# Half tiles for x, sooner loads of x, and w_v's last block in the Fourier tail of a fused FFT and expert kernel

## The chip, the cores and the metric

The kernel runs on one core of one Trainium2 chip. The metric is the time of one execution on the device in microseconds (us). A core has five engines with queues of their own: TensorE (PE, the matrix products), VectorE (DVE), ScalarE (ACT), GpSimd (POOL) and SyncE (SP), which here only issues DMAs. Each engine works through its own list in order, and waits on semaphores for the others.

## What is computed

```
X = np.fft.fft(np.fft.fft(x, axis=1), axis=2).real            # x [4, 3072, 256]
x_prev = X shifted by one place along the sequence
xk, xr = mu_k * X + (1 - mu_k) * x_prev, mu_r * X + (1 - mu_r) * x_prev
k = np.maximum(xk @ w_k, 0.0);  v = k * k @ w_v               # w_k [256, 1024], w_v [1024, 256]
r = 1.0 / (1.0 + np.exp(-(xr @ w_r)));  y = r * v             # w_r [256, 256]
h = y @ w_in;  out = (h - np.tanh(h)) @ w_out                 # w_in [256, 2048]
```

All arrays are handed over in float32, but the weights arrive as 64-bit words, which the kernel turns into float32 itself: that is the conversion of which this text speaks.

## The kernel before

**Stages.** A Fourier part (fft_phase, to about 93 us) leaves the transformed tokens in SBUF (tiles y). Phase 1 does the first expert layer for 12 blocks of 512 tokens, in 4 quads each: quad(1, ...) is a product of 2 by 2 blocks with seven instead of eight multiplications, each product made of three matmuls on split operands (mm3, L364 to L366). A quad has 7 products of the first kind (out tiles x, z, w) and, delayed by one quad, the products with w_v (out tiles o). Phase 2 does h and tanh in the same way.

**Fourier part.** x has 4 batches b of 3 pieces p, numbered here x0 to x11 (3b + p). load(b, p) (L102) fetches a piece into a tile xr with two halves, out of 3 buffers. For b below 2, one DMA on SP's queue brings both halves, and VectorE adds them (L146). For b from 2 on, SP's DMA (L110) brings the first, and a DMA on POOL's queue adds the second to it in flight (L111, "accumulating"), into half 0; half 1 of such a tile stays unused. fold_piece makes fe and fo on VectorE (L147, L148) and then issues the load of the piece three later. step1 multiplies fe and fo by the first matrix (PE L168), ScalarE spreads the result into E (L178); step2 (PE L193, ScalarE L196 to L201) and step3 (PE L234, L235, ScalarE L244, VectorE L257) make the tokens y. The loop over b and i interleaves step1 of one batch with step2 and step3 of the batch before.

**Conversion of weights.** convert (L402) yields a list of steps for each block: load of the raw words (SP, L411), absolute value (ScalarE, L433), and on VectorE the operations L421, L423, L425, L427, L429 and a sum (L437), or, for blocks that go to DRAM (wf), a store and an accumulating DMA (L444, L439). In the Fourier part four blocks of w_k (each followed by L500 to L509, which make TK), one of w_r and three of w_v stand in a list, work. more(b, i) (L286) takes steps from it: a table of rates for each b and i adds to due, and each whole number is one step. Before the last pass (b == 4) the rest of the list is emptied and the buffers of x and of the conversion are given up (fctx.close()).

**Slots.** In phase 1 and at the end of the Fourier part, side work is bound to slots: at(slot, ...) files functions, fill() runs those of the next slot. Numbering begins at -15 in the Fourier tail; quad 0 of phase 1 holds 6 fills and later quads 4, 16 slots a block. wv_task(q) gives a load of w_v's block q from wf into a tile of the 4 xk buffers, and a split: ScalarE casts it (L398) and POOL subtracts (L399). both_tasks makes the next block's left operands: d, k, the sums "+s1" to "+s4" on POOL (L669 to L672, on raw[0] to raw[3], the xk tiles) and their casts (L659) and low halves (L661). w_v's fourth block is converted in phase 1 itself (L816 to L818), the w_in blocks at places of START, the w_out blocks behind them.

**Within a quad** (L525): after the products x and z ScalarE copies s1, s2, s3; bend is ScalarE's relu (c<-z, L540), gate VectorE's square, hi the cast m (ScalarE L545), lo its low half (VectorE L547), each for four results 11, 22, 21, 12. extra() issues the product for r and gives back the sigmoid (L813), which reads the bank of x that the next quad writes first.

Of the kernel before, what the change touches and what calls it, by code (L numbers as in the profile page):

```python
# [7 lines left out]
F32 = mybir.dt.float32  # L8
# [4 lines left out]
B, S, D = 4, 3072, 256  # L13
T1, T2 = 128, 24
# [3 lines left out]
FOLDED = 2  # L18
# [69 lines left out]
def fft_phase(tc, x, f96_in, cst_in, swap, ypool, ys, work, first, hook, fill):  # L88
    nc = tc.nc
    V, A, G, T = nc.vector, nc.scalar, nc.gpsimd, nc.tensor  # L90
    ALU, ACT = mybir.AluOpType, mybir.ActivationFunctionType
    with tc.tile_pool(name="fc", bufs=1) as fc, ExitStack() as fctx, tc.tile_pool(name="fe", bufs=2) as fe, tc.tile_pool(name="fz", bufs=3) as fz, \
# [3 lines left out]
        work = work(fctx)  # L96
# [4 lines left out]
        xs = {}  # L101
        def load(b, p):  # L102
            rows = 5 if p == 2 else 4
            t = fx.tile([T1, 2, 5, D], F32, tag="xr", name=f"xr{b}_{p}")
            for c, n in FIRST[p] if b == 0 else ((0, rows),):
                src = x[:, b, :, 4 * p + c:4 * p + c + n]
                if b < FOLDED:
                    nc.sync.dma_start(out=t[:, :, c:c + n], in_=src.rearrange("k p c d -> p k c d"))
                else:
                    nc.sync.dma_start(out=t[:, 0, c:c + n], in_=src[0])  # L110
                    G.dma_start(out=t[:, 0, c:c + n], in_=src[1], accum_op=ALU.add)  # L111
            xs[b, p] = t
        zero = fc.tile([128, 128], F32, name="zero")
        V.memset(zero, 0.0)
        for b in range(B):
# [22 lines left out]
        def fold_piece(b, p):  # L138
            t = xs.pop((b, p))
            rows = 5 if p == 2 else 4  # L140
            e = fx.tile([T1, 5, 128], F32, tag="fe", name=f"fe{b}_{p}", bufs=2)
            o = fx.tile([T1, 5, 128], F32, tag="fo", name=f"fo{b}_{p}", bufs=2)
            for c, n in FIRST[p] if b == 0 else ((0, rows),):
                k = slice(c, c + n)
                if b < FOLDED:
                    V.tensor_add(t[:, 0, k], t[:, 0, k], t[:, 1, k])  # L146
                V.tensor_add(e[:, k], t[:, 0, k, 0:128], t[:, 0, k, 128:256])  # L147
                V.tensor_sub(o[:, k], t[:, 0, k, 0:128], t[:, 0, k, 128:256])  # L148
            fold[b, p] = (e, o)
            n = 3 * b + p + 3  # L150
            if n < 3 * B:
                load(*divmod(n, 3))
            if n in (4, 5):
                load_cst(n - 3)
        def step1(b, i):
# [61 lines left out]
        def step3(b, i):  # L217
            z = Z.pop((b, i))
            for k in range(2):
                chunk(b, 2 * i + k, z[:, k])  # L220
# [63 lines left out]
            return [out, back, ends]  # L284
        due = [0]
        def more(b, i):  # L286
            due[0] += 2 + (b == 2) / 2 if b else (0, 0, 2, 2, 1, 0)[i]
            for _ in range((3, 3, 2, 2, 2, 2)[i] if b == B - 1 else b == B - 2 and i > 4):
                first.pop(0)()
            while work and due[0] >= 1:  # L290
                due[0] -= 1
                work.pop(0)()
        rowjobs = []
        for b in range(B + 1):
            if b == B:
                while work:
                    work.pop(0)()
                fctx.close()
                hook()
            if b == 1:  # L300
                step3(0, 0)
            for i in range(6 if b < B else 7):
                if b < B:
                    step1(b, i)
                if b == 0:
                    if i == 5:
                        step2(0, 0)
                        step2(0, 1)
                    elif i in (1, 3):
                        warm(3)  # L310
                elif b == 1:
                    if i < 4:
                        step2(0, i + 2)
                elif i < 6 and (b < B or i == 0):
                    step2(b - 1, i)
                if rowjobs and i:
                    rowjobs.pop(0)()
                if b < 2:
                    more(b, i)
                if b == 1:  # L320
                    if i < 5:
                        step3(0, i + 1)
                    if i == 5:
                        rowjobs += upper(0)
                elif b:
                    if i == 0 and b > 2:
                        step3(b - 2, 5)
                    if b == 3 and i == 0:
                        rowjobs += upper(1)
                    if b == B and i < 5:  # L330
                        step2(b - 1, i + 1)
                    if i:
                        step3(b - 1, i - 1)
                if b > 1:
                    more(b, i)
                if b == B:
                    fill()
                    if i < 6:
                        fill()
# [1 line left out]


WARM = 9
START = (0, 8, 16, 22, 30, 38, 46)
NP = 12
TOK = 512
HID1, HID2 = 1024, 2048
# [28 lines left out]
class Kernel:  # L376
# [148 lines left out]
    def quad(self, ph, n, q, nq, S, W, w2, done, extra=None):  # L525
# [67 lines left out]
        if ph == 1:  # L593
            self.fill()
            late("t12", "g12")
        t11 = bend(Z)
        if ph == 2:
            self.fill()
        self.second(p, "22")
# [10 lines left out]
            A.copy(s3, X)  # L610
        lo("11", Z)
        self.fill()
        if r:
            r()
        if ph == 1:
            self.second(p, "21")
# [87 lines left out]
    def start1(self):  # L704

        self.sp, self.wvp = (self.ctx.enter_context(self.tc.tile_pool(name=k, bufs=1, side="right", reuse_waits="tile")) for k in ("sp", "wv"))
        self.WV = [self.wvp.tile([128, 2, TOK], F32R, tag="wv", name="wv", bufs=4) for _ in range(4)]
        self.S = [{} for _ in range(NP)]
        self.now = -15
        at = self.at  # L710
        V, raw = self.V, self.raw0
        def put(k, src):
            return self.unit(self.S[0], k, src, "S", self.G, True)
        for slot, k, src in ((-15, "a11", 0), (-14, "a12", 1), (-13, "s1", 4), (-12, "s2", 5), (-11, "s3", 2), (-10, "a22", 3), (-8, "s4", 1)):
            at(slot, *put(k, lambda i=src: raw[i]))
        at(-11, lambda: self.G.tensor_sub(raw[1], raw[1], raw[5]))
        for c, r in enumerate((self.r0, self.r1)):
            at((-7, -5)[c], lambda c=c, r=r: self.first_gate(c, r[2](), 0), lambda c=c, r=r: self.first_gate(c, r[2](), 1))
        for q in range(2):
            load, _, split = self.wv_task(q)  # L720
            at((-11, -2)[q], load)
            at((-4, 1)[q], split)

    def first_gate(self, c, src, low):
        if not low:
# [71 lines left out]
    def phase1(self):  # L797
# [14 lines left out]
            R[n, t, h] = xp.tile([128, TOK], F32, tag="r", name="r", bufs=6)  # L812
            return lambda: A.activation(R[n, t, h], ps, ACT.Sigmoid)  # L813
        at = self.at
        at(3, *self.wv_task(2))
        steps, out = self.convert(self.chunk_rows(self.wv, (3, 7)), [lambda a: self.split(self.WV[3], a, self.G)], self.x_room, V, True)  # L816
        for w, f in zip((-2, 0, 2, 6, 9, 10, 11, 13, 14), steps + out):
            at(w, f)  # L818
        free = iter([16 * n + k for n in range(6, NP) for k in (0, 2, 6, 9, 10, 11, 12, 13, 14, 15)][2:])
        for q in range(8):  # L820
            steps, out = self.convert(self.chunk_rows(self.w_out, (q, q + 8)), self.keep(12 + q), self.y_room, self.G, True)
            when = [next(free) for _ in steps[1:]]
# [12 lines left out]
        for n in range(NP):  # L835
            z = 16 * n
            if n == 0:
                for t, (f0, f1, f2) in ((4, self.r_task(0, 1, 0)), (5, self.r_task(0, 1, 1))):
                    at(t, f0, f1, f2)
            if n % 6 == 2:  # L840
                at(z + 4, lambda n=n: self.swap_rows(block(n, 1)[0]))
            if n + 1 < NP:
                u = self.both_tasks(n + 1)
                early = {0: "d0", 2: "d1", 4: "k0 d3", 5: "k1 m0", 6: "a11 d2 +0", 7: "k3 a12", 8: "k2 m1 a22"}
                rest = {9: "+s1 +1 m3", 10: "m2 s1 +s3 +3", 11: "+s2 +2", 12: "s3 +s4", 13: "s2", 14: "x0", 15: "x1", 16: "s4", 18: "x2", 19: "x3"}
                if n == 0:
                    early = {2: "d0", 3: "d1", 4: "k0", 5: "k1 m0", 6: "a11 d3 +0", 7: "d2 a12", 8: "k3 m1"}
                    rest = {**rest, 9: "k2 a22 m3 +s1", 10: "+1 m2 +s3", 11: "s1 +s2", 12: "s3 +s4 +3", 13: "s2 +2"}
                for k, names in {**early, **rest}.items():
                    for name in names.split():  # L850
                        at(z + k, u[name])
                if n % 6 == 1:
                    at(z + 12, lambda n=n: self.swap_rows(block(n + 1, 0)[0]))
            for q in range(4):
                if n + 1 == NP and q == 1:
                    self.open2()
                w2 = [[self.WV[q][:, s, 256 * c:256 * c + 256] for s in range(2)] for c in range(2)]
                k = 4 * n + q
                self.quad(1, n, q, 4, self.S[n], self.TK[q], w2, done, lambda ps: r_block(ps, k))
# [77 lines left out]
    def run(self):  # L937
        nc, tc, V = self.nc, self.tc, self.V
        ALU = mybir.AluOpType
        with tc.manual_schedule(), ExitStack() as ctx:  # L940
# [15 lines left out]
            def weights(c):  # L956
# [2 lines left out]
                wk = [c(self.quad_rows(self.wk, q, HID1 // 2), self.first_weights(self.cv, self.TK[q])) for q in range(4)]  # L959
                hi = self.WR.rearrange("p s c n -> p s (c n)")  # L960
                wr = [c(self.chunk_rows(self.wr, (0, 1)), [lambda a: self.A.copy(hi[:, 0], a), lambda a: V.tensor_sub(hi[:, 1], a, hi[:, 0].bitcast(F32))])]
                wv = [c(self.chunk_rows(self.wv, (q, q + 4)), [], None, self.wf[q]) for q in range(3)]
                todo = wk + wr + wv
                work, late = [todo[0][0][0], todo[1][0][0], todo[0][0][1]], []
                also = {1: (2,), 2: (4,)}
# [71 lines left out]
```

## Time and profile before

| | |
|---|---|
| median of 3 runs | 1648.45 us (1647.57 to 1651.6) |
| the profiled execution | 1648.89 us, span 1647.1 us |
| PE busy | 1627.6 us, 99% of the span, 7478 matmuls |
| VectorE, ScalarE, POOL busy | 1269.8, 1136.9, 585.3 us |
| DMA | 78.79 MB, 48 GB/s over the span |

In the rows below, times are us from the start of the span. A row of the timeline is one instruction or some alike in a row: start, length, engine, line, what it writes and reads; in brackets how long the engine idled before it and who ended that. Overlapping lengths are usual, since the next instruction begins before the one ahead has written its last value.

### The profile page before, as it was taken

How to read it: one execution, taken by the hardware profiler on the slowest of the kernel's cores; microseconds unless marked ns; L12 is line 12 of the kernel's file. 1: busy time of each engine (PE TensorE's matmuls, PEld its weight loads, DVE VectorE, ACT ScalarE, POOL GpSimd, SP SyncE). 2: the span in 40 equal slices, each digit the busy share in tenths (PEclk: the TensorE clock that was granted, in tenths of full speed). 3: DMA queues.
4: the chain of work that ended last, by engine and by line, in shares of the span. 5: the costliest groups of instructions: out<-in, count | busy, mean ns of one | idle time of the engine just before them, and what ended most of it. 6: DMA issues, size and time to landing. Idle time of an engine off the chain costs nothing.

```text
span 1647.1 us, 21332 instructions
## 1 busy us (share of the span) xinstructions
PE 1627.6 (99%) x7478; PEld 1345.5 (82%) x7478; DVE 1269.8 (77%) x1958; ACT 1136.9 (69%) x2167; POOL 585.3 (36%) x496
## 2 busy tenths in 40 slices
PE   8999999999999999999999999999999999999998
PEld 7977888888878887888888888888888888888887
DVE  8978888888888887777777777777777777777776
ACT  5887777777777777776666666666666666666665
POOL 0266667665667766462121212121212121202000
PEclk9999999999999999999999999999999999999999
DMA  9711111111111102201010101010101010101000
GB/s 331 189 37 39 47 39 46 45 46 58 46 65 64 40 32 97 90 26 52 1 52 1 51 1 51 1 52 1 52 1 52 1 52 1 52 1 52 4 23 26
DMA packets 39468, 78.79 MB, mean 48 GB/s; under 512 B 4656, under 2 KB 11696, under 8 KB 39360
## 3 DMA queue, kind: packets, MB, share of 16 engines
q1 hardware_dynamic: 37344, 72.44, 13.0%
q0 software_dynamic: 1296, 4.19, 1.5%
q8 instruction: 58, 0.95, 0.2%
q10 hardware_dynamic: 720, 0.79, 0.1%
q14 instruction: 50, 0.41, 0.1%
HBM read 46.41 MB, written 31.00 MB: 47 GB/s over the span
## 4 chain that ended last, share of the span: by engine, by line
PE 89%; DVE 4%; ACT 3%; DMA 2%; issue 1%; POOL 0%; SPq 0%; ACTq 0%; DVEq 0%; POOLq 0%
PE o L366 15%; PE o L365 15%; PE o L364 15%; PE x L364 8%; PE x L366 8%; PE x L365 7%; PE w L364 4%; PE w L365 4%; PE w L366 4%; PE z L364 2%; PE z L366 2%; PE z L365 2%; DMA xr<-x 1%; PE r L366 1%; PE r L364 1%
## 5 line engine op out<-in xcount | busy, mean ns | idle before, releaser
L661 POOL TENSOR_TENSOR a<-xk,a 128x512 fp32r<-128x512 f32 x72 | 94.0, 1307 | 596.1 <-ACT a L659 596.1
L547 DVE TENSOR_TENSOR m<-z,m 128x512 fp32r<-128x512 f32 x288 | 198.5, 689 | 137.4 <-ACT m L545 137.4
L365 PE MATMUL o<-m,WO 128*128 128x512 f32 x768 | 298.9, 389 | 0.0
L366 PE MATMUL o<-m,WO 128*128 128x512 f32 x768 | 298.8, 389 | 0.0
L364 PE MATMUL o<-m,WO 128*128 128x512 f32 x768 | 298.8, 389 | 0.0
L540 ACT ACTIVATE c<-z 128x512 f32<-128x512 f32 x288 | 172.9, 600 | 146.1 <-DVE z L625 145.3
L545 ACT CAST m<-z 128x512 fp32r<-128x512 f32 x288 | 169.2, 587 | 145.4 <-DVE z L629 81.7
L661 POOL TENSOR_TENSOR s<-xk,s 128x512 fp32r<-128x512 f32 x94 | 123.8, 1318 | 187.2 <-ACT s L659 185.2
L365 PEld LDWEIGHTS o<-m,WO 128*128 128x128 f32 x768 | 144.2, 188 | 30.2 <-DVE m L547 0.3
L364 PEld LDWEIGHTS o<-m,WO 128*128 128x128 f32 x768 | 144.2, 188 | 30.0
L366 PEld LDWEIGHTS o<-m,WO 128*128 128x128 f32 x768 | 144.2, 188 | 29.8
L629 DVE TENSOR_TENSOR z<-z,c 128x512 f32<-128x512 f32 x144 | 100.6, 698 | 69.4 <-ACT c L540 69.4
L366 PE MATMUL o<-m,wv 128*128 128x512 f32 x384 | 149.6, 390 | 0.1
L364 PE MATMUL o<-m,wv 128*128 128x512 f32 x384 | 149.6, 390 | 0.0
L365 PE MATMUL o<-m,wv 128*128 128x512 f32 x384 | 149.5, 389 | 0.0
L562 ACT COPY s<-x 128x512 f32<-128x512 f32 x144 | 84.9, 590 | 55.8 <-PE x L366 55.6
L583 ACT COPY s<-x 128x512 f32<-128x512 f32 x144 | 84.6, 588 | 53.9 <-PE x L366 53.4
L625 DVE TENSOR_TENSOR z<-w,s 128x512 f32<-128x512 f32 x143 | 99.8, 698 | 25.2 <-PE w L366 9.8
L600 DVE TENSOR_TENSOR z<-z,c 128x512 f32<-128x512 f32 x144 | 100.3, 696 | 24.1 <-ACT c L540 23.4
L651 DVE TENSOR_TENSOR x<-x,c 128x512 f32<-128x512 f32 x144 | 99.5, 691 | 7.4 <-ACT c L540 7.0
L652 DVE TENSOR_TENSOR c<-c 128x512 f32<-128x512 f32 x96 | 67.3, 701 | 49.3 <-ACT c L540 49.3
L547 DVE TENSOR_TENSOR m<-x,m 128x512 fp32r<-128x512 f32 x144 | 98.8, 686 | 2.6
(217 smaller groups left out, 4039.5 us busy)
## 6 DMA issues: line engine op xcount, KB each, us to landing
spill<-r SPq DMA_DIRECT2D x48, 256.0 KB
xk<-spill SPq DMA_DIRECT2D x48, 256.0 KB
out<-o SPq DMA_DIRECT2D x22, 512.0 KB
raw<-w_in SPq DMA_DIRECT2D x32, 128.0 KB
cv<-w_out SPq DMA_DIRECT2D x16, 256.0 KB
wf<-wf SPq DMA_DIRECT2D x16, 256.0 KB
xr<-x SPq DMA_DIRECT2D x3, 1024.0 KB
xr<-x SPq DMA_DIRECT2D x5, 512.0 KB
```

The source lines that it names most:

```text
L364: T.matmul(ps, w[0], m[0], start=start, stop=False, skip_group_check=True)
L365: T.matmul(ps, w[0], m[1], start=False, stop=False, skip_group_check=True)
L366: T.matmul(ps, w[1], m[0], start=False, stop=stop, skip_group_check=True)
L540: A.activation(t, src, ACT.Tanh if ph == 2 else ACT.Relu)
L545: A.copy(M[blk][:, 0], g)
L547: V.tensor_sub(M[blk][:, 1], g, M[blk][:, 0].bitcast(F32))
L562: A.copy(s1, X)
L600: gate(Z, Z, t11)
L625: V.tensor_add(Z, Wb, s3)
L629: gate(Z, Z, t22)
L651: g21=lambda: gate(X, X, st["t21"]), h21=lambda: hi("21", X), l21=lambda: lo("21", X),
L661: eng.tensor_sub(S[name][:, 1], src(), S[name][:, 0].bitcast(F32))
```

## The change

1. *x.* From b = 2 on two pieces share one tile xr, one in each half: x6 and x7, x8 and x9, x10 and x11. The loads go out as: x7 and x8 behind the fold of x4, and then one piece behind each further fold (x9 behind x5's).
2. *more.* Its rates are (0, 0, 0, 2, 1, 2) in batch 0, 1.75 in batches 1 and 3 for 2, and in batch 3 it leaves four steps in the list, which are emptied behind the first step2 of the last pass.
3. *w_v's last block* is converted in the Fourier part like the other three and comes to phase 1 as they do, by a load at slot 10 and a split at slot 12; the other three blocks' loads and splits move by one to three slots.
4. *The first sigmoid* stands behind the first relu instead of behind lo.
5. *START* goes up by one, the list of free places begins one later, and in block 0 "a12" moves from slot 7 to 8.

PE's list of instructions is the same before and after. In the changed file the lines behind load are 3 to 7 further on (L147 is L150, L398 is L403, L659 is L666).

**VectorE, from the first conversion operation to the fold of x4.** xr_0 and fe_0 here are x3, xr_1 and fe_1 x4; cva is the absolute value of a block. Before:

```order
L421 TENSOR_SCALAR cva<-cva 128x512
L423 TENSOR_SCALAR cva<-cva 128x512
L425 SCALAR_TENSOR_TENSOR cva<-raw,cva 128x512
L427 TENSOR_SCALAR cvs<-cva 128x512
L429 SCALAR_TENSOR_TENSOR cvb<-raw,cvs 128x512
L437 TENSOR_TENSOR cva<-cva,cvb 128x512
L146 TENSOR_TENSOR xr_0_170<-xr_0_170 128x1024
L147 TENSOR_TENSOR fe_0_243<-xr_0_170 128x512
L148 TENSOR_TENSOR fo_0_244<-xr_0_170 128x512
```

After:

```order
L426 TENSOR_SCALAR cva<-cva 128x512
L428 TENSOR_SCALAR cva<-cva 128x512
L149 TENSOR_TENSOR xr_0_170<-xr_0_170 128x1024
L150 TENSOR_TENSOR fe_0_235<-xr_0_170 128x512
L151 TENSOR_TENSOR fo_0_236<-xr_0_170 128x512
L430 SCALAR_TENSOR_TENSOR cva<-raw,cva 128x512
L432 TENSOR_SCALAR cvs<-cva 128x512
L434 SCALAR_TENSOR_TENSOR cvb<-raw,cvs 128x512
L442 TENSOR_TENSOR cva<-cva,cvb 128x512
L426 TENSOR_SCALAR cva<-cva 128x512
L428 TENSOR_SCALAR cva<-cva 128x512
L149 TENSOR_TENSOR xr_1_177<-xr_1_177 128x1024
```

The four last operations of the first block moved from ahead of the fold of x3 to behind it.

**SyncE's queue, the loads from x6 on.** Before, xr_0, xr_1, xr_2 are the pieces of batch 2 (x6, x7, x8) and then of batch 3; after, xr_0_240 holds x6 and x7, xr_2_323 x8 and x9, xr_1_472 x10 and x11. Before:

```order
L110 DMA xr_0_248<-x 128x1024
L411 DMA raw<-wk 128x256 x4
L110 DMA xr_1_321<-x 128x1024
L411 DMA raw<-wk 128x256 x4
L110 DMA xr_2_400<-x 128x1280
L411 DMA raw<-wr 128x512 x2
L110 DMA xr_0_473<-x 128x1024
L411 DMA raw<-wv 128x512 x2
L110 DMA xr_1_527<-x 128x1024
```

After:

```order
L113 DMA xr_0_240<-x 128x1024
L416 DMA raw<-wk 128x256 x4
L113 DMA xr_0_240<-x 128x1024
L113 DMA xr_2_323<-x 128x1280
L113 DMA xr_2_323<-x 128x1024
L416 DMA raw<-wk 128x256 x4
L416 DMA raw<-wr 128x512 x2
L113 DMA xr_1_472<-x 128x1024
L416 DMA raw<-wv 128x512 x2
L113 DMA xr_1_472<-x 128x1280
```

The loads of x8 and x9 moved ahead of the last wk block, that of x9 with it ahead of wr.

**ScalarE in quad 0 of phase 1.** s are the copies, c<-z the relu, m its cast, r the sigmoid. Before:

```order
L589 COPY s<-x 128x512
L419 ACTIVATE cva<-raw 128x512
L540 ACTIVATE c<-z 128x512
L545 CAST m_1209<-z 128x512
L398 CAST wv<-wv 128x512
L813 ACTIVATE r<-r 128x512
```

After:

```order
L594 COPY s<-x 128x512
L545 ACTIVATE c<-z 128x512
L820 ACTIVATE r<-r 128x512
L550 CAST m_1215<-z 128x512
L545 ACTIVATE c<-z 128x512
L403 CAST wv<-wv 128x512
```

The sigmoid moved ahead of m and of the cast of w_v, and the absolute value is gone from this place.

**ScalarE in quad 3 of phase 1**, from the second copy s on (L583 before, L588 after). Before:

```order
L583 COPY s<-x 128x512
L659 CAST s_1503<-xk 128x512
L540 ACTIVATE c<-w 128x512
L540 ACTIVATE c<-z 128x512
L545 CAST m_1520<-w 128x512
```

After:

```order
L588 COPY s<-x 128x512
L403 CAST wv<-wv 128x512
L666 CAST s_1502<-xk 128x512
L545 ACTIVATE c<-w 128x512
L545 ACTIVATE c<-z 128x512
L550 CAST m_1519<-w 128x512
```

The cast of w_v's last block stands between the copy and the cast of the next left operand.

```diff
--- before.py
+++ after.py
@@ -101,15 +101,18 @@
         xs = {}
         def load(b, p):
             rows = 5 if p == 2 else 4
-            t = fx.tile([T1, 2, 5, D], F32, tag="xr", name=f"xr{b}_{p}")
+            half = (3 * b + p) % 2 if b >= FOLDED else 0
+            if not half:
+                xs["last"] = fx.tile([T1, 2, 5, D], F32, tag="xr", name=f"xr{b}_{p}")
+            t = xs["last"]
             for c, n in FIRST[p] if b == 0 else ((0, rows),):
                 src = x[:, b, :, 4 * p + c:4 * p + c + n]
                 if b < FOLDED:
                     nc.sync.dma_start(out=t[:, :, c:c + n], in_=src.rearrange("k p c d -> p k c d"))
                 else:
-                    nc.sync.dma_start(out=t[:, 0, c:c + n], in_=src[0])
-                    G.dma_start(out=t[:, 0, c:c + n], in_=src[1], accum_op=ALU.add)
-            xs[b, p] = t
+                    nc.sync.dma_start(out=t[:, half, c:c + n], in_=src[0])
+                    G.dma_start(out=t[:, half, c:c + n], in_=src[1], accum_op=ALU.add)
+            xs[b, p] = t[:, half:half + 2 - (b >= FOLDED)]
         zero = fc.tile([128, 128], F32, name="zero")
         V.memset(zero, 0.0)
         for b in range(B):
@@ -148,8 +151,9 @@
                 V.tensor_sub(o[:, k], t[:, 0, k, 0:128], t[:, 0, k, 128:256])
             fold[b, p] = (e, o)
             n = 3 * b + p + 3
-            if n < 3 * B:
-                load(*divmod(n, 3))
+            for k in {7: (7, 8)}.get(n, (n + (n > 7),)):
+                if k < 3 * B:
+                    load(*divmod(k, 3))
             if n in (4, 5):
                 load_cst(n - 3)
         def step1(b, i):
@@ -284,19 +288,14 @@
             return [out, back, ends]
         due = [0]
         def more(b, i):
-            due[0] += 2 + (b == 2) / 2 if b else (0, 0, 2, 2, 1, 0)[i]
+            due[0] += (0, 1.75, 2.5, RATE, 0)[b] if b else (0, 0, 0, 2, 1, 2)[i]
             for _ in range((3, 3, 2, 2, 2, 2)[i] if b == B - 1 else b == B - 2 and i > 4):
                 first.pop(0)()
-            while work and due[0] >= 1:
+            while len(work) > (4 if b == B - 1 else 0) and due[0] >= 1:
                 due[0] -= 1
                 work.pop(0)()
         rowjobs = []
         for b in range(B + 1):
-            if b == B:
-                while work:
-                    work.pop(0)()
-                fctx.close()
-                hook()
             if b == 1:
                 step3(0, 0)
             for i in range(6 if b < B else 7):
@@ -325,6 +324,11 @@
                 elif b:
                     if i == 0 and b > 2:
                         step3(b - 2, 5)
+                    if b == B and i == 0:
+                        while work:
+                            work.pop(0)()
+                        fctx.close()
+                        hook()
                     if b == 3 and i == 0:
                         rowjobs += upper(1)
                     if b == B and i < 5:
@@ -341,7 +345,8 @@
 
 
 WARM = 9
-START = (0, 8, 16, 22, 30, 38, 46)
+RATE = 1.75
+START = (1, 9, 17, 23, 31, 39, 47)
 NP = 12
 TOK = 512
 HID1, HID2 = 1024, 2048
@@ -594,6 +599,8 @@
             self.fill()
             late("t12", "g12")
         t11 = bend(Z)
+        if r:
+            r()
         if ph == 2:
             self.fill()
         self.second(p, "22")
@@ -610,7 +617,7 @@
             A.copy(s3, X)
         lo("11", Z)
         self.fill()
-        if r:
+        if r and p:
             r()
         if ph == 1:
             self.second(p, "21")
@@ -718,8 +725,8 @@
             at((-7, -5)[c], lambda c=c, r=r: self.first_gate(c, r[2](), 0), lambda c=c, r=r: self.first_gate(c, r[2](), 1))
         for q in range(2):
             load, _, split = self.wv_task(q)
-            at((-11, -2)[q], load)
-            at((-4, 1)[q], split)
+            at((-8, -2)[q], load)
+            at((-2, 2)[q], split)
 
     def first_gate(self, c, src, low):
         if not low:
@@ -812,11 +819,9 @@
             R[n, t, h] = xp.tile([128, TOK], F32, tag="r", name="r", bufs=6)
             return lambda: A.activation(R[n, t, h], ps, ACT.Sigmoid)
         at = self.at
-        at(3, *self.wv_task(2))
-        steps, out = self.convert(self.chunk_rows(self.wv, (3, 7)), [lambda a: self.split(self.WV[3], a, self.G)], self.x_room, V, True)
-        for w, f in zip((-2, 0, 2, 6, 9, 10, 11, 13, 14), steps + out):
-            at(w, f)
-        free = iter([16 * n + k for n in range(6, NP) for k in (0, 2, 6, 9, 10, 11, 12, 13, 14, 15)][2:])
+        for q in (2, 3):
+            at((4, 10)[q - 2], *self.wv_task(q))
+        free = iter([16 * n + k for n in range(6, NP) for k in (0, 2, 6, 9, 10, 11, 12, 13, 14, 15)][3:])
         for q in range(8):
             steps, out = self.convert(self.chunk_rows(self.w_out, (q, q + 8)), self.keep(12 + q), self.y_room, self.G, True)
             when = [next(free) for _ in steps[1:]]
@@ -844,7 +849,7 @@
                 early = {0: "d0", 2: "d1", 4: "k0 d3", 5: "k1 m0", 6: "a11 d2 +0", 7: "k3 a12", 8: "k2 m1 a22"}
                 rest = {9: "+s1 +1 m3", 10: "m2 s1 +s3 +3", 11: "+s2 +2", 12: "s3 +s4", 13: "s2", 14: "x0", 15: "x1", 16: "s4", 18: "x2", 19: "x3"}
                 if n == 0:
-                    early = {2: "d0", 3: "d1", 4: "k0", 5: "k1 m0", 6: "a11 d3 +0", 7: "d2 a12", 8: "k3 m1"}
+                    early = {2: "d0", 3: "d1", 4: "k0", 5: "k1 m0", 6: "a11 d3 +0", 7: "d2", 8: "k3 m1 a12"}
                     rest = {**rest, 9: "k2 a22 m3 +s1", 10: "+1 m2 +s3", 11: "s1 +s2", 12: "s3 +s4 +3", 13: "s2 +2"}
                 for k, names in {**early, **rest}.items():
                     for name in names.split():
@@ -959,7 +964,7 @@
                 wk = [c(self.quad_rows(self.wk, q, HID1 // 2), self.first_weights(self.cv, self.TK[q])) for q in range(4)]
                 hi = self.WR.rearrange("p s c n -> p s (c n)")
                 wr = [c(self.chunk_rows(self.wr, (0, 1)), [lambda a: self.A.copy(hi[:, 0], a), lambda a: V.tensor_sub(hi[:, 1], a, hi[:, 0].bitcast(F32))])]
-                wv = [c(self.chunk_rows(self.wv, (q, q + 4)), [], None, self.wf[q]) for q in range(3)]
+                wv = [c(self.chunk_rows(self.wv, (q, q + 4)), [], None, self.wf[q]) for q in range(3)] + [c(self.chunk_rows(self.wv, (3, 7)), self.keep(3))]
                 todo = wk + wr + wv
                 work, late = [todo[0][0][0], todo[1][0][0], todo[0][0][1]], []
                 also = {1: (2,), 2: (4,)}
```

## Rows read from the trace of the kernel before

**Rows 1.** Windows of the span: busy time (instructions) by engine, clock, DMA share, GB/s.

```profile
core 0: us, PE busy (x) PEld busy (x) DVE busy (x) ACT busy (x) POOL busy (x), PEclk, DMA share, GB/s
0.00:20.00 20.00, 13.61 (x98) 12.69 (x99) 12.85 (x33) 7.15 (x24) 0.20 (x4) 1.00 0.93 336
20.00:50.00 30.00, 28.56 (x257) 27.29 (x256) 29.11 (x59) 22.18 (x75) 4.34 (x6) 1.00 1.01 320
50.00:93.00 43.00, 41.12 (x360) 39.54 (x359) 34.55 (x72) 37.01 (x113) 16.23 (x21) 1.00 0.57 128
93.00:160.00 67.00, 63.78 (x269) 48.90 (x268) 57.08 (x82) 49.57 (x93) 41.68 (x33) 1.00 0.12 40
160.00:800.00 640.00, 638.30 (x2790) 520.00 (x2789) 523.38 (x786) 471.92 (x874) 393.39 (x333) 1.00 0.15 51
```

**Rows 2.** Timeline of PE in the Fourier part, first matmuls behind its gaps.

```profile
16.74 0.94 PE L168 MATMUL s<-f,fo 128*128 128x128 f32 x6 [1.14 <-ACT E L178]
...
34.59 0.83 PE L168 MATMUL s<-f,fe 128*128 128x128 f32 x6
...
39.58 1.13 PE L168 MATMUL s<-f,fe 128*128 128x128 f32 x8 [1.26 <-DVE fe L147]
...
52.28 0.91 PE L168 MATMUL s<-f,fe 128*128 128x128 f32 x6 [0.89 <-DVE fe L147]
...
60.21 1.13 PE L168 MATMUL s<-f,fe 128*128 128x128 f32 x8 [0.63 <-DVE fe L147]
```

**Rows 3.** PE's waits from 93 to 165: us in total, times, longest.

```profile
PE x L364 <- ACT r L813: 1.3, 1, 1.3
PE x L364 <- ACT s L562: 0.9, 3, 0.3
PE w L364 <- DVE z L625: 0.5, 1, 0.5
PE z L364 <- DVE m L547: 0.4, 1, 0.4
```

**Rows 4.** Timeline of VectorE in the Fourier part.

```profile
17.05 0.69 DVE L425 SCALAR_TENSOR_TENSOR cva<-raw,cva 128x512 int32<-128x512 int32 x1
...
19.67 1.23 DVE L146 TENSOR_TENSOR xr<-xr 128x1024 f32<-128x1024 f32 x1
...
23.01 1.22 DVE L146 TENSOR_TENSOR xr<-xr 128x1024 f32<-128x1024 f32 x1
...
51.31 0.83 DVE L147 TENSOR_TENSOR fe<-xr 128x640 f32<-128x640 f32 x1 [1.53 <-DMA xr<-x]
...
88.08 1.18 DVE L257 TENSOR_TENSOR y<-pe,pq 128x360 f32<-128x360 f32 x4 [4.39 <-ACT pe L244]
```

**Rows 5.** The chain that ended last, around piece x8: start, us, what.

```profile
34.45 7.89 DMA xr<-x
...
42.90 8.32 DMA xr<-x
```

**Rows 6.** Timeline of ScalarE, the first sigmoid.

```profile
100.99 0.60 ACT L813 ACTIVATE r<-r 128x512 f32<-128x512 f32 x1
```

**Rows 7.** Timelines of POOL, ScalarE, VectorE and PE in quad 3.

```profile
131.86 1.29 POOL L671 TENSOR_TENSOR xk<-xk 128x512 f32<-128x512 f32 x1
...
132.38 0.63 ACT L659 CAST s<-xk 128x512 fp32r<-128x512 f32 x1
...
134.89 0.69 DVE L547 TENSOR_TENSOR m<-w,m 128x512 fp32r<-128x512 f32 x1
...
136.42 0.39 PE L364 MATMUL w<-s,TK 128*128 128x512 f32 x1
```

**Rows 8.** A load of w_v, the window behind it, and landing of stores to wf.

```profile
95.60 0.33 SPq L701 DMA_DIRECT2D wv<-wf  x1
...
98.00:99.00 1.00, 1.00 (x6) 0.80 (x5) 0.70 (x1) 1.00 (x3) 0.00 (x0) 1.00 0.00 0
...
DMA to landing us min/median/max: 3.9/4.0/4.1
```

**Rows 9.** Waits of all engines from 128 to 143, PE's weight loads.

```profile
PEld o L366 <- POOL wv L399: 0.5, 1, 0.5
```

## Prediction

> **What bounds the kernel now.** I read the table by windows first: TensorE (PE) is busy in all but 19.4 of 1647 us, at a granted clock of 1.00 in every stretch (2.4 GHz), so a change that leaves PE's instructions alone moves only its gaps [rows 1]. Of these 19.4 us, 6.39 lie in the first 20 us, most of them ahead of anything the change touches, and 4.8 behind 800 us, at the end. Open are some 8 us: 1.44 from 20 to 50, 1.88 to 93, 3.22 to 160, 1.70 to 800. Second, which producer ended each gap. In the Fourier part: A, 1.14, ScalarE's E copy; C 1.26, D 0.89 and F 0.63, all VectorE's fold (fe); and E, the 0.36 that is left of the 1.88 [rows 1, 2]. In phase 1 the largest, 1.3, ended with the first sigmoid; three waits for s add up to 0.9, two for VectorE's z and m are 0.5 and 0.4 [rows 3]. Third, VectorE itself: 29.11 of the 30 us from 20 to 50 are busy, so a fold there comes as late as the work queued ahead of it; only at 51.31 did it wait 1.53 for x [rows 1, 4]. And the DMA share is 0.93 and 1.01 up to 50 us: a transfer that starts sooner takes its room from another [rows 1].
>
> **The profiled execution** took 1648.89 us with a span of 1647.1; the sum is made against it. The median of the three runs is 1648.45, 0.44 lower.
>
> **Part 1, absolute value and conversion later.** In A, ScalarE's E copies stood behind the absolute value of weight block 0, which waited for its load. At i=3 it stands behind them: A closes but for 0.1, and PE is 1.05 earlier from 16.7 on. VectorE pays. Before, all six conversion operations of block 0 ran ahead of the fold of x piece 3, which began at 19.67 without a wait. Now the last four, 17.05 to 19.67, are behind that fold, and it could begin at 17.0 if x3 were there. The trace only shows that x3 had landed by 19.67. By bytes: 6.2 MB are asked for up to x3 (0.1 + 3.4 + 0.6 + 1.05 + 1.05: first matrix, batch 0, constants, two weight blocks, x3) and 6.7 MB (20 x 336) had moved by 20 us, so not before 20 x 6.2 / 6.7 = 18.5 [rows 1, 4]. It shares its last stretch with x4, so I take 19.3, nearer the row. VectorE then idles 2.3 us, and fold 4 finds ahead of it what was there before (23.01 - 19.67 = 3.34), 0.37 sooner, and the four operations (2.62): 25.26, **2.25 later**. Counted in the order, conversion ahead of fold 5 is 1.25 us less than before, of fold 6 1.1, of fold 7 1.4, of fold 8 1.85, of folds 9 to 11 1.7. So folds 5 and 6 come 1.0 and 1.1 late, fold 8 is back at about 50.3 if x is there.
>
> PE, step by step [rows 2, 4]: it took x5's fe at 34.59, some 0.9 us after the fold had made it. With A closed it asks at 33.54 and gets it at about 34.8: the 1.05 is gone and PE is 0.2 late. Batch 2 starts with x6's fe, 1.1 later than 39.58: 40.7. From there to batch 3 are 60.21 - 39.58 = 20.63 us, 1.88 of it D, E and F. It asks for x8's fe at 51.39 + 1.1 = 52.5; the old fold 8 has it by 52.14, so D closes. At batch 3 it stands at 59.4 if E and F close too, and at 60.2 if fold 9 still ends then. Half way: **-0.45 us**, between -1.0 (x3 at 18.8) and +0.8 (the tail, part 3).
>
> **Part 2, x sooner.** Before, x8's copy ran from 34.45 to 42.34, and its accumulating DMA on POOL's queue from 42.90 to 51.22 [rows 5]. Now x7 and x8 go out behind fold 4, and x9 behind them, all ahead of the last wk block and wr on SP's queue. That block's first operation on VectorE now stands behind fold 7, so it has cover. What x8 gains is D, counted already: **0**.
>
> **Part 3, w_v's last block in the tail.** Its six operations are 3.4 us of VectorE (those of block 0 took 16.12 to 19.67), and 1.8 come over from part 1. VectorE idled 4.39 there ahead of 88.08, and PE's gaps from 50 to 93 are all ahead of 61 [rows 1, 2, 4]. 5.2 on 4.4: it costs nothing if 0.8 of it fits beside, up to 0.8 if not. **0.**
>
> **Part 4, quad 0.** The sigmoid began at 100.99, behind an absolute value, the cast m and a cast of w_v; its 0.60 ended as PE's 1.3 us wait did [rows 3, 6]. Of these only c<-z stays ahead of it: with casts of 0.63 [rows 7] it is 1.3 to 1.8 us sooner, and the wait is gone. The cast of w_v also leaves the place ahead of the first s, 0.26 of the 0.9. **-1.55.**
>
> **Part 5, quads 1 and 2.** The block's VectorE and ScalarE work leaves phase 1; the waits for z and m, 0.9, lose it, and of the 0.6 left of s I take none [rows 3]. **-0.9.** Without a new wait PE's w<-s of 136.42 would run 2.45 sooner, at 133.97.
>
> **Part 6, the new wait.** w_v's last block now comes by a load (slot 10) and a split (slot 12). Its buffer is that of raw[3], which POOL's +s2 (L671) reads last, until 133.15 [rows 7]. I put POOL's row 3.1 us sooner, 2.45 as PE and the rest from its own waits for VectorE: the load starts at T = 130.05, give or take 0.8. A like load of 256 KB, issued at 95.60, had no packets left by 98.0: 2.4. The accumulating stores of that size took 3.9 to 4.1 from issue to landing [rows 8]. I take 3.1, between: 133.15. On ScalarE the cast of that block stands right behind s (L583), where the s3 cast was (132.38 before, 129.9 now). So **ScalarE waits about 3 us**, and behind it the s3 cast, c<-w, c<-z and m<-w. Before, from that cast to the end of VectorE's m (135.58), which frees the bank for PE's w<-s, it took 3.20 [rows 7]. With the new cast (0.52) and 0.12 to PE: 133.15 + 3.84 = 137.0 for 133.97, **+3.05**. PE's weight load that waited 0.5 for POOL's half of that block [rows 9] waits no more, and some of it was PE's own time: **-0.3**.
>
> On the landing the Trainium skill ("DMA: Bandwidth & Descriptors", Anatomy of one DMA) gives a transfer 2.0 us plus its bytes at 436 GB/s; for 256 KB that is 2.6 us, an estimate. The rows above have 3.9 to 4.1 for accumulating stores and at least 2.4 for a load; by 2.6 the total would be 0.5 us lower.
>
> **Part 7, w_in one place on.** PE's 1.70 us of gaps from 160 to 800 are short ones [rows 1]. One place is a sixteenth of a block's slots; some gaps go, others may come. Between -1.5 (nearly all of them) and +0.3 (as much as one more such gap) I take the middle, **-0.6**.
>
> **Sum:** -0.45 - 1.55 - 0.9 + 3.05 - 0.3 - 0.6 = -0.75; 1648.89 - 0.75 = **1648.1 us**.
>
> **Rivals.**
> 1. *The wait for w_v is hidden.* If +s2 ends some 3 us sooner still, the 3.05 falls away: 1645.1. For it: POOL holds fewer operations ahead of it and VectorE beside it is relieved. Against: from the end of +s2 at 133.15 to PE's w<-s at 136.42 are 3.3 us, and load, cast and chain need 6.9 [rows 7].
> 2. *x sooner closes everything.* A, C, D, E and F are 4.28: for -0.45 that gives 1644.3. It needs fold 6 on time, and so x3 by 17. For it: VectorE is the only one in C. Against: x3's bytes, above.
> 3. *The early copies crowd the accumulates* (slower). x8 and x9 (1.2 MB, 3.6 us at 320 GB/s) now move beside x6's and x7's accumulates with the DMA share at 1.01 [rows 1]. x8's accumulate had landed 0.1 us ahead of fold 8 [rows 4, 5]; PE asks at 52.5, so a slip of over 0.4 decides. With 3.4, x8's fe comes at 55.5 and batch 3 at 62.4 for 59.8: 1648.1 + 2.7 = 1650.8. Against: the last wk block and wr, 1 MB, which moved there before, are behind them now. The Trainium skill (same page, Queues, rings and completion order) states that an engine takes turns between its queues packet by packet, which speaks for it; the trace shows one share near 1 and not whose packets went first.
> 4. *The sooner sigmoid only hands its gap to the next z*: part 4 gives 0.3 instead of 1.55: 1649.4.
>
> **How the numbers follow.** Forecast 0.50, rival 1 0.18, rival 2 0.07, rival 3 0.17, rival 4 0.08. The range runs from just under rival 1 to rival 3 and its bounds: 1644.7 to 1651.2. 0.3% is 4.9 us, about what a measurement of this kernel can tell from no change: faster needs less than 1643.5, rivals 1 and 2 together, 0.06; slower more than 1653.4, rival 3 with w_v at its upper bounds, 0.05; within, 0.89.
>
> **What would show it.** Right: no gap of PE near 15.4; VectorE idle about 2 us ahead of the fold of x3; batch 2 on PE near 40.7; no wait for the sigmoid near 101; ScalarE waiting for a DMA of w_v near 130 and a PE gap of 2 to 3 us at w<-s. Wrong: no such wait (rival 1), batch 2 before 39.6 (rival 2), folds 6 to 8 waiting for x (rival 3), a z behind the sigmoid (rival 4). New gaps of PE behind 160 us would make the whole sum wrong.

## The result, and the profile after

The changed kernel takes 1658.24 us (median of 6 runs, 1657.41 to 1658.83) for 1648.01 of the kernel before: a ratio of 1.0059, interval 1.0046 to 1.0071. It is slower by 10.2 us, and lies outside the range of the forecast. Its profiled execution has a span of 1656.7 us, 9.6 more than that of before. PE's instructions are the same, so one matmul's start can be compared with itself.

The windows of the changed kernel, columns as in [rows 1]:

```profile
core 0: us, PE busy (x) PEld busy (x) DVE busy (x) ACT busy (x) POOL busy (x), PEclk, DMA share, GB/s
0.00:20.00 20.00, 15.12 (x106) 14.18 (x106) 10.61 (x29) 7.91 (x28) 0.20 (x4) 1.00 0.93 338
20.00:50.00 30.00, 26.57 (x220) 24.80 (x220) 26.63 (x52) 16.50 (x55) 4.50 (x6) 0.94 1.05 331
50.00:93.00 43.00, 42.03 (x367) 40.16 (x365) 42.49 (x77) 40.15 (x123) 13.14 (x18) 1.00 0.52 126
93.00:160.00 67.00, 54.17 (x225) 43.80 (x226) 46.30 (x67) 41.58 (x79) 37.04 (x31) 0.90 0.09 28
160.00:800.00 640.00, 639.10 (x2808) 525.04 (x2807) 528.58 (x795) 475.40 (x881) 400.68 (x338) 1.00 0.16 53
```

PE lost 12.8 of the 67 us from 93 to 160 (3.2 before), and there and from 20 to 50 the clock column is below 1.00. The two levels stand apart in short windows of the same trace:

```profile
42.00:44.00 2.00, 2.00 (x12) 2.00 (x11) 1.97 (x5) 0.71 (x3) 0.00 (x0) 0.50 1.06 235
103.00:105.00 2.00, 2.00 (x11) 2.00 (x10) 0.55 (x2) 0.97 (x2) 0.00 (x0) 0.50 0.78 269
151.00:153.00 2.00, 2.00 (x6) 1.52 (x6) 1.11 (x2) 1.30 (x3) 2.00 (x3) 0.50 0.00 0
```

These lie behind the three long stops of PE. The timeline of PE, at its stops and at some matmuls named below (in brackets idle time and releaser):

```profile
34.76 0.91 PE L172 MATMUL s<-f,fe 128*128 128x128 f32 x6 [0.92 <-DVE fe L150]
...
41.24 1.84 PE L172 MATMUL s<-f,fe 128*128 128x128 f32 x8 [2.37 <-DVE fe L150]
...
61.94 1.16 PE L172 MATMUL s<-f,fe 128*128 128x128 f32 x8 [0.27 <-ACT ex L187]
...
101.73 0.82 PE L239 MATMUL pq<-cst,zt 128*128 128x144 f32 x2 [9.27 <-DVE y L261]
...
106.65 0.49 PE L369 MATMUL x<-a,TK 128*128 128x512 f32 x1
...
113.50 0.39 PE L369 MATMUL x<-a,TK 128*128 128x512 f32 x1
...
140.25 0.39 PE L369 MATMUL z<-a,TK 128*128 128x512 f32 x1
...
149.66 0.50 PE L369 MATMUL w<-s,TK 128*128 128x512 f32 x1 [3.13 <-DVE m L552]
...
156.85 0.39 PE L369 MATMUL z<-a,TK 128*128 128x512 f32 x1
```

| the same matmul | before | after | behind by | new in this piece |
|---|---|---|---|---|
| batch 3, first of step1 | 60.21 | 61.94 | 1.73 | Fourier part +1.73 |
| pq behind the stop | 90.39 | 101.73 | 11.34 | tail +9.61 |
| phase 1, first x<-a | 93.02 | 106.65 | 13.63 | half clock behind it +2.29 |
| next quad, first x<-a | 101.64 | 113.50 | 11.86 | first sigmoid -1.77 |
| z<-a of quad 3 | 130.15 | 140.25 | 10.10 | quads 1, 2 -1.76 |
| w<-s of quad 3 | 136.42 | 149.66 | 13.24 | wait for w_v +3.14 |
| z<-a of quad 4 | 142.22 | 156.85 | 14.63 | half clock +1.71, then -0.32 |
| end of the span | 1647.1 | 1656.7 | 9.6 | all the rest -5.0 |

VectorE's rows of the changed kernel show the tail's stop (beside [rows 4]):

```profile
19.41 1.23 DVE L149 TENSOR_TENSOR xr<-xr 128x1024 f32<-128x1024 f32 x1 [2.40 <-DMA xr<-x]
...
25.26 1.22 DVE L149 TENSOR_TENSOR xr<-xr 128x1024 f32<-128x1024 f32 x1
...
40.40 0.69 DVE L150 TENSOR_TENSOR fe<-xr 128x512 f32<-128x512 f32 x1 [0.46 <-DMA xr<-x]
...
86.92 10.48 DVE L426 TENSOR_SCALAR cva<-cva 128x512 f32<-128x512 f32 x1
97.44 0.43 DVE L428 TENSOR_SCALAR cva<-cva 128x512 int32<-128x512 int32 x1
```

L426, the clamp of w_v's last block, takes 10.48 us, 25 times the 0.42 that is the median of its 13 executions. Behind it stand the block's five other operations (3.0 us) and then y's puts, which give PE its bank pq back. POOL's rows beside it:

```profile
86.97 2.83 POOL L668 TENSOR_TENSOR a<-xk,a 128x512 fp32r<-128x512 f32 x2
89.43 2.83 POOL L668 TENSOR_TENSOR s<-xt,s 128x512 fp32r<-128x512 f32 x2
91.90 1.57 POOL L723 TENSOR_TENSOR xk<-xk,xt 128x512 f32<-128x512 f32 x1
93.11 1.57 POOL L668 TENSOR_TENSOR s<-xk,s 128x512 fp32r<-128x512 f32 x1
94.33 1.56 POOL L668 TENSOR_TENSOR a<-xk,a 128x512 fp32r<-128x512 f32 x1
95.56 1.55 POOL L668 TENSOR_TENSOR s<-xk,s 128x512 fp32r<-128x512 f32 x1
```

Eight operations follow one another from 86.97 to 97.11 without a break; the clamp ends 0.29 behind the last. An estimate from these rows: with the clamp 10.06 us shorter, PE would have had pq at 91.67, before it asked for it (101.73 - 9.27 = 92.46), so the clamp alone accounts for the whole stop.

The wait for w_v in quad 3 (beside [rows 7]), POOL's +s2 and ScalarE's cast:

```profile
141.95 1.31 POOL L678 TENSOR_TENSOR xk<-xk 128x512 f32<-128x512 f32 x1
...
145.89 0.62 ACT L403 CAST wv<-wv 128x512 fp32r<-128x512 f32 x1 [3.44 <-DMA wv<-wf]
```

+s2 ended at 143.26, the load began then, and the cast waited 3.44 for it.

### The profile page after: what moved, and what is told of

Same layout as the page of the kernel before. It is cut to its first block, busy times and chain, and to the rows that moved or that the text cites. A ratio compares the mean times of both kernels' runs of the same rounds, so it can differ in the third digit from the quotient of the medians.

```text
span 1656.7 us, 21330 instructions
## 1 busy us (share of the span) xinstructions
PE 1629.2 (98%) x7478; PEld 1353.0 (82%) x7478; DVE 1274.5 (77%) x1958; ACT 1137.8 (69%) x2167; POOL 587.5 (35%) x496
## 4 chain that ended last, share of the span: by engine, by line
PE 89%; POOL 1%; ACT 0%; issue 0%; DVE 0%; DMA 0%; ACTq 0%; POOLq 0%
PE o L370 15%; PE o L371 15%; PE o L369 15%; PE x L369 8%; PE x L370 8%; PE x L371 8%; PE w L369 4%; PE w L370 4%; PE w L371 4%; PE z L369 2%; PE z L371 2%; PE z L370 2%; PE r L370 1%; PE r L369 1%; PE r L371 1%
## 5 line engine op out<-in xcount | busy, mean ns | idle before, releaser
L588 ACT COPY s<-x 128x512 f32<-128x512 f32 x144 | 84.6, 588 | 54.2 <-PE x L371 53.3
L659 DVE TENSOR_TENSOR c<-c 128x512 f32<-128x512 f32 x96 | 67.3, 701 | 49.3 <-ACT c L545 49.3
```

## The experiments

Times are medians; beside each stands the ratio to the kernel before with its interval.

**1. Part 3 undone** (in the changed kernel).

```diff
-wv = [... for q in range(3)] + [c(self.chunk_rows(self.wv, (3, 7)), self.keep(3))]
+wv = [... for q in range(3)]       # list emptied ahead of the last pass; block converted in phase 1
```

> The changed kernel with part 3 undone: w_v's last block is converted in phase 1 as before, the list is emptied ahead of the last pass. Theory: the tail's stop of 9.3 us and its half clock (2.0 us) and the wait for w_v's load in quad 3 (3.5 and 1.5) all hang on part 3 and go; the block's work returns to quads 1 and 2 (up to +1.5). 1658.2 - 16.3 + 0.9 = 1642.8. Rival: the conversion deferred by the new rates keeps VectorE late in the tail too, and a stop of 2 us or more stays at 94 us: 1648 or more.

1645.86 us, 0.9983 (0.9973 to 0.9992). The stop of the tail, the wait in quad 3 and the half clock behind each are gone: part 3 cost 12.4 us, with its return to phase 1 counted. The theory's sum was 3 us too good. The block's return costs more than its 0.9: from phase 1's first x<-a to quad 3's z<-a PE gained 1.2 us on the kernel before, for 3.5 in the changed kernel. The profiled execution was also 1.3 us behind the changed kernel's already at 21 us; and it has the gap (2.10) and the half clock near 42 too, which are not part 3's.

**2. The clamp in another form.**

```diff
-V.tensor_scalar(a, a, LOW, HIGH, op0=ALU.max, op1=ALU.min)
+V.scalar_tensor_tensor(a, a, LOW, high_tile_broadcast, op0=ALU.max, op1=ALU.min)
```

> The changed kernel; in w_v's last block the clamp (one SBUF operand and two numbers, 0.43 us, but 10.48 us beside POOL's run of 87 to 97 us) is one with two SBUF operands, the upper bound read from a tile. Theory P1: the form with one operand is what POOL's unbroken run keeps out; with two operands it comes in at the next change of POOL's instructions, within 2 us: the stop of 9.3 us and its clock go, 1658.2 - 11 = 1647. Theory P2: POOL's run keeps out any VectorE operation that reads SBUF alone: the clamp takes 10 us again and the time stays at 1658. Rival Q: the 10.48 us are no contention but a wait inside for data: it stays as well, and then another order of the same form helps as little.

1673.85 us, 1.0156 (1.0139 to 1.0173). The tail answers the question, VectorE's clamp and POOL's last operation:

```profile
87.23 10.45 DVE L428 SCALAR_TENSOR_TENSOR cva<-cva,lim 128x512 f32<-128x512 f32 x1
...
95.58 1.54 POOL L672 TENSOR_TENSOR s<-xk,s 128x512 fp32r<-128x512 f32 x1
```

10.45 us in the other form, ending 0.56 behind POOL's run: P1 is out. P2 and Q are both still possible. The time of the whole misled (experiment 8).

**3. POOL's run shortened.**

```diff
-return self.unit(self.S[0], k, src, "S", self.G, True)
+return self.unit(self.S[0], k, src, "S", V if k in ("s3", "a22", "s4") else self.G, True)
```

> The changed kernel; three of the eight operations of POOL's run from 87 to 97 us (the low halves of s3, a22 and s4) are made by VectorE behind y's puts, so that the run is about 6.2 us long. Theory P2: POOL's unbroken run keeps VectorE's clamp out as long as it lasts, so the clamp, first in line from 86.9, ends at about 93.6 for 97.4 and takes 6.7 us: the stop of PE shortens from 9.3 to about 5.5, 1658.2 - 3.8 + 0.5 for VectorE's three operations = 1655. Rival Q: the clamp waits for something of its own and takes 10.5 us again: 1658 or more.

1655.13 us, 1.0042 (1.0028 to 1.0056). VectorE's clamp, POOL's run of five, and PE's stop:

```profile
87.13 6.59 DVE L426 TENSOR_SCALAR cva<-cva 128x512 f32<-128x512 f32 x1
...
86.95 2.83 POOL L668 TENSOR_TENSOR a<-xk,a 128x512 fp32r<-128x512 f32 x2
89.42 2.80 POOL L668 TENSOR_TENSOR s<-xt,s 128x512 fp32r<-128x512 f32 x2
91.87 1.56 POOL L723 TENSOR_TENSOR xk<-xk,xt 128x512 f32<-128x512 f32 x1
...
98.06 0.82 PE L239 MATMUL pq<-cst,zt 128*128 128x144 f32 x2 [5.38 <-DVE y L261]
```

The run ends at 93.43, the clamp at 93.72, after 6.59 us; PE's stop is 5.38. The clamp's data, form and place are those of the changed kernel, only POOL's run differs. The clamp is 3.89 us shorter and so is PE's stop, so Q falls: VectorE was shut out for as long as POOL's run lasted. The Trainium skill ("SBUF — State Buffer", SBUF: two separate sides) describes the port pair that VectorE and GpSimd share as an exclusive lock, held for a whole instruction while the other is fully blocked. The traces agree, with one addition: it was not one instruction of 1.2 us that blocked, but five or eight.

**4. w_v's last block into a free buffer.**

```diff
-at((4, 10)[q - 2], *self.wv_task(q))          # q = 3: an xk buffer, slot 10
+at(4, load3)                                  # tile tag "cva" of xp; split at slot 12 as before
```

> The changed kernel; w_v's last block is loaded into a buffer that nobody else uses by then, at slot 4 for 10, and split at slot 12 as before. Theory: the 3.13 us of PE at w<-s in quad 3 are the load that starts only behind POOL's +s2; with it gone they go, and the 3.4 us of half clock behind them (1.5 us): 1658.2 - 4.6 = 1653.6. Rival: POOL's chain would be as late without the load, and PE waits 1 us or more at the same place: 1655 to 1657.

1654.34 us, 1.0040 (1.0025 to 1.0055), 3.9 less than the changed kernel. ScalarE's s copy and the cast:

```profile
141.79 0.59 ACT L588 COPY s<-x 128x512 f32<-128x512 f32 x1 [1.06 <-PE x L371]
142.27 0.62 ACT L403 CAST wv<-wv 128x512 fp32r<-128x512 f32 x1
```

The cast follows the copy at once, and PE's wait for m at w<-s is gone. Part 6's mechanism holds.

**5. The places alone** (in the kernel before).

```diff
-START = (0, 8, 16, 22, 30, 38, 46)            # and free[2:]
+START = (1, 9, 17, 23, 31, 39, 47)            # and free[3:]
```

> The kernel before with the conversion places of w_in and w_out one place on, and nothing else. Theory S: this alone gives what the changed kernel gained between 160 and 700 us, where matmul for matmul it fell from 14.2 to 10.0 us behind the kernel before: 1648.0 - 4.1 = 1643.9. Rival: the gain there comes from the other edits, and the shift is worth what the listed gaps of 1.7 us allow: 0 to -1.2, 1647.4. S wants PE's 4.1 us to go in stalls of about 0.2 us, below what the list of gaps shows, at the places where a matmul starts 0.43 behind its predecessor for 0.23.

1644.3 us, 0.9975 (0.9966 to 0.9985): 4.1 us, theory S. The list of PE's gaps couldn't show it: a matmul's row is 0.39 long and the next starts 0.23 later, so a stall of up to 0.16 leaves no gap. The waits of PE's weight loads (us in total, times, longest) from 160 to 480 do show it. Before:

```profile
PEld z L364 <- DVE m L547: 5.6, 18, 0.8
PEld x L364 <- ACT s L562: 1.4, 6, 0.2
```

With the places moved:

```profile
PEld z L364 <- DVE m L547: 1.4, 8, 0.2
PEld x L364 <- ACT s L562: 0.8, 2, 0.6
```

**6. The Fourier part's two halves, each alone** (in the kernel before): the loads of x, then the rates of conversion.

```diff
+for k in {7: (7, 8)}.get(n, (n + (n > 7),)):  # with half tiles, as in the change
```

> The kernel before with the half tiles and sooner loads of x alone. Theory: x8's accumulate is there sooner, D (0.89) closes, and the accumulates of x6 and x7, which now share their room with x8's and x9's copies, land up to 3 us later: C stays or grows by up to 0.5. 1648.4 - 0.9 + 0.5 = 1648.0. Rival: the accumulates are crowded so far that folds 6 or 7 wait over 1 us, and half clock follows: 1650 or more.

```diff
-due[0] += 2 + (b == 2) / 2 if b else (0, 0, 2, 2, 1, 0)[i]
+due[0] += (0, 1.75, 2.5, 1.75, 0)[b] if b else (0, 0, 0, 2, 1, 2)[i]
```

> The kernel before with the new rates of conversion alone (first absolute value at i=3). Theory: gap A closes, VectorE idles 2.4 us ahead of the fold of x3, C grows from 1.26 to about 2, and PE falls to half clock for 3.4 us behind it (1.7 us): batch 3 starts about 1.5 us later, 1649.5 to 1650. Rival: the loss in the Fourier part (1.76 us at batch 3) is that of the loads, and the rates alone bring the forecast -0.45: 1648.0.

1649.78 us, 1.0012 (1.0003 to 1.0021), and 1649.72 us, 1.0011 (1.0002 to 1.0020): each loses, 1.8 and 1.7 us. With the loads alone, the fold of x6 waits for its accumulating DMA, which takes 8.3 us for 5.8 before:

```profile
40.59 0.69 DVE L150 TENSOR_TENSOR fe<-xr 128x512 f32<-128x512 f32 x1 [1.32 <-DMA xr<-x]
...
xr<-x POOLq DMA_DIRECT2D x1, 512.0 KB, 8.3
```

With the rates alone (PE's rows), x5's fe and batch 2 come late:

```profile
35.09 0.91 PE L168 MATMUL s<-f,fe 128*128 128x128 f32 x6 [0.96 <-DVE fe L147]
...
41.02 2.05 PE L168 MATMUL s<-f,fe 128*128 128x128 f32 x8 [1.82 <-DVE fe L147]
```

Both times a gap near 41 us of 1.8 to 2.5 us was followed by 3.4 us at half clock. In the changed kernel x6's accumulate took 8.7 us, and its fold waited 0.46 only because VectorE was itself late.

That the gap and its half clock are what each half costs is not shown. At batch 3 PE was 0.94 us behind the trace of before with the loads alone, and 0.39 with the rates alone, for the 1.5 that was expected. The five traces with an unchanged Fourier part (before, and experiments 5, 7 and 8) begin batch 3 anywhere from 59.12 to 61.18, and in the first one of experiment 7 the same gap was 2.01 us and half clock followed it there too:

```profile
40.41 1.64 PE L168 MATMUL s<-f,fe 128*128 128x128 f32 x8 [2.01 <-DVE fe L147]
```

In the trace of the loads alone, PE ran another 3.4 us at half clock in quad 0, behind a wait of 1.78 us for the sigmoid. Two things do stand clear of this spread: x6's accumulate took 5.7 to 7.8 us in the six traces with the old loads and 8.3 to 8.7 in the six with the sooner ones, and the five traces with both halves begin batch 3 at 61.94 to 63.24.

**7. Places and sigmoid**, first with the new slots of w_v and a12, then without (kernel before).

```diff
+if r:                                         # behind t11 = bend(Z); later only if r and p
+    r()
```

> The kernel before with parts 4 and 7: the first sigmoid behind the first relu, the loads and splits of w_v's first three blocks at the new slots, the conversion places one on, a12 at slot 8. Nothing of the Fourier part or of w_v's last block is changed. If the edits add up: 1644.3 for the places alone, less the 1.3 us of the sigmoid's wait and 0.26: 1642.7. Rival: the sooner sigmoid hands its gap to the next z, since w_v's last block is still converted in quads 0 to 3: 1644.

> The kernel before with the conversion places one on and the first sigmoid behind the first relu; the loads and splits of w_v and a12 stay where they were. In the run with the new slots PE stopped 1.3 us at about 121 for POOL's low half of xr, which stood behind a split of w_v 2.7 us later than before. Theory: with the old slots that stop goes: 1643.1 - 1.2 = 1641.9. Rival: the old slot of the cast of w_v in quad 0 gives back the 0.26 and delays m as before, and nothing is gained: 1643.

1643.12 us, 0.9969 (0.9959 to 0.9980), and 1643.49 us, 0.9968 (0.9956 to 0.9981): the fastest versions, about 5 us below the kernel before, not told apart from one another; the 1641.9 expected of the second did not come. That the sigmoid adds to the 4.1 of the places is not shown: the two gain about 0.8 and 1.2 us more than experiment 5, less than the intervals can tell. In the trace with the new slots PE waits 0.88 us, at 121.27, for POOL's low half of xr, behind the later splits of w_v. With the old slots that wait is gone, and PE has none for the sigmoid, but this one:

```profile
103.89 0.50 PE L364 MATMUL x<-s,TK 128*128 128x512 f32 x1 [1.53 <-ACT s L562]
```

1.53 for 0.29 before: as long as w_v's last block is converted in quad 0, what the sooner sigmoid gave PE (1.5 us at the next quad's first x<-a) is lost again by this x<-s. That was rival 4, here, though not in the changed kernel, where that work is gone (-1.77).

**8. Four bytes** (in the kernel before).

```diff
+self.lim = self.w1.tile([128, 1], F32, name="lim")    # behind WR, set once, never read
```

> The kernel before with one unused tile of 4 bytes a partition behind WR, which moves every later tile on that side of SBUF by 4 bytes, and a memset of it. In the run with the other clamp the same tile stood there, and from 693 us on matmuls came 0.006 us later each in rows of about 40, some 15 us in all. Theory: the displaced operands cost that, whatever the clamp: 1648.0 + 15 = 1663. Rival: the clamp's form or its reads cost it, and the tile costs nothing: 1648.

1663.88 us, 1.0092 (1.0073 to 1.0110). It costs 15 us, and experiment 2 had the same tile: so most of its excess goes with the tile and not with the clamp. Its trace agrees: at 600 us PE was 0.4 us behind the changed kernel, at the end 15.

## Why the prediction was wrong

- **Part 3 failed.** It weighed VectorE's 5.2 us of work against 4.4 idle and took the operations at the length that they have in a quiet place (the clamp at 0.43). It didn't ask what POOL does in that idle time, and none of its rivals does. The first and the last row of POOL's run in the trace of before stood there to be read:

```profile
84.02 2.50 POOL L661 TENSOR_TENSOR a<-xk,a 128x512 fp32r<-128x512 f32 x2 [2.63 <-ACT a L659]
...
92.65 1.28 POOL L661 TENSOR_TENSOR s<-xk,s 128x512 fp32r<-128x512 f32 x1
```

  VectorE's operations beside that run were y's puts, which read one operand from SBUF and one from PE's bank, and were not held up (1.18 us for four, [rows 4]). One that worked on SBUF alone was: 1.87 us for the 0.84 of the same operation at 95.33, ending 0.55 behind the run:

```profile
92.61 1.87 DVE L730 TENSOR_TENSOR xr<-xt,xr 128x512 fp32r<-128x512 f32 x1 [1.00 <-ACT xr L727]
```

  The price was 9.6 us and 2.3 of half clock, for 0.
- **Part 1** had the mechanism: VectorE idle 2.40 ahead of x3 (forecast 2.3), fold 4 at 25.26 (25.26), x5's fe at 34.76 (34.8), batch 2 at 41.24 (40.7), D closed. Left out were 0.46 for x6's accumulate, and the half clock behind a 2.37 us gap, 1.6 us. So it came to +1.73 at batch 3 for -0.45; that figure is of single executions, which differ there by up to 2 us without any change (experiment 6).
- **Part 2 failed** at its 0: the accumulates of x6 to x9 took 8.7 to 11.2 us, for 5.8 to 9.3 before. Rival 3's mechanism is there, at x6 and not x8.
- **Part 4** (-1.55 to -1.77) held, **part 5** brought -1.76 for -0.9. The waits for s, of which it took none, went too; and the -1.76 holds a new stop that no part has, 0.90 us at 132.86 for POOL's low half of xr, which cost 1.1. The later splits of w_v's first blocks bring it (experiment 7: there with the new slots, gone with the old).
- **Part 6** held in its cause: PE's stop was 3.13 for 3.05. That the size fits so well is in part luck: from +s2's end to the cast it took 2.6 for 3.1, and PE would have asked for w<-s 3.27 behind that end (149.66 - 3.13 - 143.26) for 3.92, so two misses cancelled. The estimate of 2.6 from the Trainium skill ("DMA: Bandwidth & Descriptors", Anatomy of one DMA) was the nearer one, though that section's fit is of DMAs that POOL issues and this load is SP's. The clock behind the stop, another 1.7, was left out.
- **Part 7** was mis-sized: -0.6 forecast, about -4 measured alone. The step that failed is the bound by the listed gaps, 1.70.

The large gain of part 7 hid a still larger loss: without it the change would cost some 14 us.

## What to carry to other kernels

Before an operation goes into an engine's idle time, read what the engine with which it shares a port does then: here a run of ready POOL operations held a VectorE operation that works on SBUF alone until the run's end, and everything queued behind it paid. For a full PE, read the waits of its weight loads beside its gaps. Where a change opens a new stop of PE, look for a lower clock behind it and add what it takes: here 1.6 to 2.3 us more.

## What the runs showed of the hardware

- Three stops of PE, of 2.4, 9.3 and 3.1 us, were followed by PEclk 0.50 (1.2 GHz) in stretches of about 3.4, 4.6 (of busy time) and 3.4 us, worth 1.6, 2.3 and 1.7 us. Before the stops PE had been busy; a gap of 1.26 at the place of the first, in the kernel before, left 1.00, and so did one of 1.62 in experiment 8. A stop does not explain every fall: in experiment 5's trace 3.4 us at half clock begin at 18.9 us, and PE's stops in the 8 us ahead are of 1.2 us at most.
- An unused tile of 4 bytes a partition ahead of other tiles cost 15 us. Matmuls from 700 to 1600 us are 0.003 to 0.004 us longer in the mean; the kernel with the tile, then before (busy us, mean ns):

```profile
L366 PE MATMUL o<-m,WO 128*128 128x512 f32 x696 | 273.3, 393 | 0.0
```

```profile
L366 PE MATMUL o<-m,WO 128*128 128x512 f32 x706 | 274.6, 389 | 0.0
```

  That the tile works by moving later tiles, and which operand would mind, was not tried.
